# A spare PSUM column for the row maximum, the query ratio on GpSimd, and a strict order of all operations

## The chip, the cores and the metric

The kernel runs on one core of a Trainium2 chip. Five engines work side by side, each through its own queue in order: the matmul engine (PE, with its weight loads PEld), VectorE (DVE), ScalarE (ACT), GpSimd (POOL) and SyncE (SP), which issues most of the transfers. Data lies in SBUF, and matmuls write to PSUM, of which this kernel uses four tiles of two banks each. The metric is the device time of one execution in microseconds, as the median of several runs.

## The reference

A transformer layer on 2048 rows of 640: a linear attention with a learned feature map, then a bilinear gated FFN, each behind a layer norm and with a residual.

```python
x = A_x
h = x + _A_ref(_layernorm(x), A_wqkv, A_w_phi, A_wo)
h2 = h + _B_ref(_layernorm(h), B_w_gate, B_w_up, B_w_down)

# _A_ref, 32 heads of 20:
qkv = x @ wqkv                                # q, k, v
pq, pk = q @ w_phi[h], k @ w_phi[h]           # 20 x 20 per head
phi_q = concat(softmax(pq), softmax(-pq))     # 40 features
phi_k = concat(softmax(pk), softmax(-pk))
kv = sum_s phi_k[s] v[s];  z = sum_s phi_k[s]
o = (phi_q @ kv) / (phi_q @ z + 1e-6);  return o @ wo
# _B_ref: ((x @ w_gate) * (x @ w_up)) @ w_down, 1536 wide
```

## The kernel before

The 2048 rows are 16 tiles t of 128. Work is recorded as operations in named units, each on one engine; names carry the tile number.

- `s`: sums for the layer norm of a batch of tiles (PE and DVE, for batch s12 ACT squares), ending on POOL with `rs`, the reciprocal root (line 600). `x`, `y`: the key and query weights times w_phi. `c`: the value weights centred. `wo`: means of Wo's rows.
- `k`t: the key projection (ten matmuls of 128x320 into a PSUM tile), then `softexp`: DVE takes the negated largest magnitude of the row (`mx`, line 730) and multiplies it by `rs` (`nb`, line 733, both one column per partition), and ACT writes two exponentials, of plus and minus the row, with `nb` as bias (line 737). `K`t: DVE sums each group of 20 (line 748) and takes reciprocals (750), and POOL scales the key features with them (751).
- `v`t: the value projection, moved to SBUF by ACT. `A`t: the KV products of two tiles; all of them gather in one PSUM tile, which DVE moves to SBUF in unit `Aout` (817, 820).
- `q`t: query projection and `softexp`, into one of three `eq` buffers. `Q`t: DVE sums (770), a reciprocal (775) and the ratio of the two softmax sums (`rq`, line 776), then POOL scales half of the features with the ratio (781), and two DMA transposes bring them to `phiqT`.
- `n`t: the numerators, divided by DVE (848, 849) and transposed (by PE for tiles 0 and 1, else by DMA). `h`t: the product with Wo; DVE adds the residual (865 makes the mean column `mh`, 868 the sum), then a transpose, and the sum of squares on ACT and POOL.
- `f`b.i.j: FFN columns i for four tiles of block b (two tiles in block 0): five matmuls for the gate and five for the up half into the two banks of a PSUM tile; ACT copies the gate half (889), DVE multiplies (891). `d`t and `e`t: the product with w_down, scaling, residual and store.

Each row tile up to the KV eviction passes through PE, DVE, ACT and POOL; every numerator needs the KV product of all sixteen. From the first FFN unit on, PE has long runs of matmuls.

Which operation stands where on an engine is set when the program is built. `ORDER` lists unit names for each engine as ranks, and `Prog.place` walks through time with planned durations (`t`, `lat` of each operation): of the first four to six operations of an engine's list (`AHEAD`) it takes the first that can start by about the earliest possible time. Buffers from pools, the four PSUM tiles (`p_ps`) among them, are given out in that walk; a tile comes free when the last operation that names it in `use` has ended. The finished program has fixed queues, with semaphore waits where an operation needs another engine's result.

Of the kernel before, what the change touches and what calls it, by code (L numbers as in the profile page):

```python
# [5 lines left out]
FP32 = mybir.dt.float32  # L6
BF16 = mybir.dt.bfloat16
ACT = mybir.ActivationFunctionType
ALU = mybir.AluOpType
AX = mybir.AxisListType  # L10
# [26 lines left out]

SC = 175.0 / 128.0
# [23 lines left out]
    "DVE":  # L62
# [8 lines left out]
    "ACT":  # L71
# [7 lines left out]
    "POOL":  # L79
# [38 lines left out]
class Prog:  # L118
# [6 lines left out]
    AHEAD = {"PE": 4, "DVE": 6, "ACT": 6, "POOL": 4, "SP": 6}  # L125

    def __init__(self, nc, ctx):
        self.nc, self.ctx = nc, ctx
        self.ops = []
        self.rings = {}  # L130
        self.unit = None
        self.rank = {}
# [48 lines left out]
    def place(self):  # L181
# [3 lines left out]
        for o in ops:  # L185
            for d in o.deps:
                d.succ.append(o)
            o.open = len(o.deps)
            o.start = None
        free = {e: 0.75 for e in self.ENGS}  # L190
        fabric = 0.0
        for o in ops:
            self.rank.setdefault((o.eng, o.unit), len(self.rank))
        queue = {e: sorted((o for o in ops if o.eng == e), key=lambda o: (self.rank[e, o.unit], o.n)) for e in self.ENGS}
        flight = {}
        order = []
        wide = False
        while len(order) < len(ops):
            best = None
            for e in self.ENGS:  # L200
                cand, seen = [], 0
                for o in queue[e]:
                    if seen >= self.AHEAD[e] and not (wide and not cand):
                        break
                    seen += 1
                    if o.open:
                        continue
                    s = max([free[e]] + [d.end + (0.05 if d.eng != e else 0.0) for d in o.deps
                                         if d.eng != e or d.dma is not None or e not in ("PE", "SP")])
                    ok = True  # L210
                    for b in o.bufs:
                        if b.i is None:
                            if not b.pool.free:
                                ok = False
                                break
                            s = max(s, min(b.pool.free_at[j] for j in b.pool.free))
                    if ok and o.dma is not None:
                        fl = flight.get(o.dma[0], [])
                        if len(fl) >= o.dma[1]:
                            s = max(s, fl[-o.dma[1]])  # L220
                    if ok:
                        cand.append((s, o))
                if not cand:
                    continue
                s0 = min(c[0] for c in cand)
                s, o = next(c for c in cand if c[0] <= s0 + 0.06)
                if best is None or s < best[0]:
                    best = (s, o)
            if best is None:
                if wide:  # L230
                    raise RuntimeError("nothing can be placed")
                wide = True
                continue
            wide = False
# [25 lines left out]
            queue[o.eng].remove(o)  # L260
# [109 lines left out]
def _build(ctx, nc, A_x, A_wqkv, A_w_phi, A_wo, B_w_gate, B_w_up, B_w_down, out):  # L370
    g = Prog(nc, ctx)

    def sb(shape, dt, name):
        return ctx.enter_context(nc.sbuf_tensor(name, shape, dt))
# [37 lines left out]
    mx = sb([P, 2 * NT], FP32, "mx")  # L412
# [316 lines left out]
    def softexp(v, t, i, dst, regs_, use=()):  # L729
        g.op("DVE", lambda e: e.tensor_reduce(out=mx[:, i:i + 1], in_=PS[v.i][:, :, 0:HALF], axis=AX.XY, op=ALU.max,  # L730
                                              apply_absolute_value=True, negate=True), rd=v.R, wr=[R_mx[i]], use=[v],
             t=0.735, lat=0.85)
        g.op("DVE", lambda e: e.tensor_tensor(out=nb[:, i:i + 1], in0=mx[:, i:i + 1], in1=rs[:, t:t + 1], op=ALU.mult),  # L733
             rd=[R_mx[i], R_rs[t]], wr=[R_nb[i]], t=0.1, lat=0.2)
        for s in range(2):
            sc = rs if s == 0 else nrs
            g.op("ACT", lambda e, s=s, sc=sc: e.activation(  # L737
                out=signed(dst(), s), in_=PS[v.i][:, :, 0:HALF].rearrange("p b (h f) -> p b h f", f=DH), func=ACT.Exp,
                bias=nb[:, i:i + 1], scale=sc[:, t:t + 1]), rd=v.R + [R_nb[i], R_rs[t], R_nrs[t]], wr=[regs_[s]], use=[v] + list(use),
                t=0.775, lat=0.92)  # L740
# [21 lines left out]
    def queries(t, after=()):  # L762
# [10 lines left out]
        def sums(k):  # L773
            return Sq[:, vs.i, :].rearrange("p (h s) -> p h s", s=2)[:, :, k]
        g.op("DVE", lambda e: e.reciprocal(out=rq[:, vr.i, :], in_=sums(1)), rd=vs.R, wr=vr.R, use=[vs, vr], t=0.26, lat=0.38)
        g.op("DVE", lambda e: e.tensor_tensor(out=rq[:, vr.i, :], in0=sums(0), in1=rq[:, vr.i, :], op=ALU.mult),  # L776
             rd=vs.R + vr.R, wr=vr.R, use=[vs, vr], t=0.11, lat=0.2)
# [220 lines left out]
    for e, names in ORDER.items():  # L998
        for i, n in enumerate(names.split()):
            g.rank[e, n] = i  # L1000
# [29 lines left out]
```

## Time and profile before

| | |
|---|---|
| median of 3 runs | 298.22 us (298.15 to 298.28) |
| profiled execution | 298.66 us, its span 296.9 us |
| PE busy | 282.0 us, 2346 matmuls |
| DVE busy | 185.7 us, 302 instructions |
| ACT busy | 136.8 us |
| POOL busy | 104.6 us |
| granted TensorE clock, mean | 0.994 |

The span runs from the first to the last instruction; the profiled time has 1.8 us around it. In the page's rows stand the line, engine and operation, what is written and read, shapes and count; then busy time and the mean of one, and the engine's idle time just before with what ended it. In the window rows each engine has its busy time and its count; behind them stand the granted clock (1.00 is full speed), the share of the DMA engines and GB/s. Rows of waits give the total in us, how often, and the longest. Most tiles are parts of larger buffers, so names repeat: the FFN's matmuls show as `phik,Wgu`, since their input lies in the buffer that held the keys.

### The profile page before, as it was taken

What the parts mean: (1) busy time and instruction counts of PE and PEld (TensorE: products, weight loads), DVE (VectorE), ACT (ScalarE), POOL (GpSimd) and SP (SyncE); (2) the same over time, 40 slices, a digit from 0 to 9 for tenths busy, and PEclk for the clock granted to TensorE, in tenths of its full rate; (3) what the DMA queues carried; (4) which work ended last, traced back from release to release, by engine and by line L of the source; (5) the groups of instructions that cost most, each with busy time, mean ns of one, the idle gap of its engine ahead of it and who ended that gap; (6) DMA issues with size and microseconds to landing.
All of it is one profiled execution on the core that took longest, in us unless ns stands there. A gap on an engine that the chain in (4) does not pass through costs nothing.

```text
span 296.9 us, 5723 instructions
## 1 busy us (share of the span) xinstructions
PE 282.0 (95%) x2346; PEld 192.5 (65%) x2357; DVE 185.7 (63%) x302; ACT 136.8 (46%) x226; POOL 104.6 (35%) x143
## 2 busy tenths in 40 slices
PE   8999999787967999999999999999999999999996
PEld 8877677464866788978765466667654444456773
DVE  0799999999997989988775657352213232323201
ACT  1457897667834856526445213253332323223121
POOL 8426898663861154041252200151540000001042
PEclk9999999999998999999999999999999999999999
DMA  7978999600162587525434412518120000001111
GB/s 196 198 102 166 186 343 374 240 0 0 24 93 64 165 214 111 92 66 112 101 56 112 90 44 46 92 44 129 50 66 2 0 0 0 2 0 44 46 44 66
DMA packets 65193, 28.08 MB, mean 95 GB/s; under 512 B 55696, under 2 KB 63888, under 8 KB 65168
## 3 DMA queue, kind: packets, MB, share of 16 engines
q1 hardware_dynamic: 64240, 27.37, 40.7%
q10 hardware_dynamic: 928, 0.35, 0.5%
q8 instruction: 18, 0.29, 0.4%
q14 instruction: 7, 0.06, 0.1%
HBM read 11.82 MB, written 2.62 MB: 49 GB/s over the span
## 4 chain that ended last, share of the span: by engine, by line
PE 72%; DVE 21%; issue 3%; DMA 1%; POOL 1%; SPq 0%; ACT 0%; DVEq 0%; ACTq 0%; POOLq 0%
PE ps L553 71%; DVE Ssum L748 6%; DVE mx L730 4%; DVE nb L733 3%; DVE Rk L750 2%; DVE Sq L770 1%; DMA phiqT<-eq 1%; DVE rq L776 1%; PE ps L636 1%; DVE ob L849 1%; DVE Wp L684 0%; POOL eq L781 0%; DVE sxx L590 0%; DVE t L587 0%; SPq L462 0%
## 5 line engine op out<-in xcount | busy, mean ns | idle before, releaser
L553 PE MATMUL ps<-phik,Wgu 128*128 128x512 bf16 (+1 forms) x590 | 105.3, 336 | 0.5
L553 PEld LDWEIGHTS ps<-phik,Wgu 128*128 128x128 bf16 x600 | 58.3, 98 | 44.7 <-issue 0.2
L553 PE MATMUL ps<-Wp,xT 128*128 128x320 bf16 x480 | 69.9, 301 | 3.8 <-ACT eq L737 2.3
L891 DVE TENSOR_TENSOR phik<-ps,gate 128x512 bf16<-128x512 f32 (+1 forms) x60 | 34.8, 583 | 51.6 <-PE ps L553 50.5
L889 ACT ACTIVATE gate<-ps 128x512 bf16<-128x512 f32 (+1 forms) x60 | 30.6, 512 | 73.1 <-PE ps L553 73.1
L553 PE MATMUL ps<-vaug,phik 128*128 128x320 bf16 (+3 forms) x543 | 60.6, 273 | 2.3 <-POOL phik L751 2.2
L553 PEld LDWEIGHTS ps<-Wp,xT 128*128 128x128 bf16 x480 | 45.9, 98 | 22.9 <-ACT eq L737 3.0
L553 PEld LDWEIGHTS ps<-vaug,phik 128*128 128x128 bf16 x544 | 44.3, 100 | 18.2 <-POOL phik L751 2.4
L907 POOL TENSOR_TENSOR outb<-t,x_all 128x640 bf16<-128x640 f32 x12 | 16.7, 1397 | 83.2 <-ACT t L904 79.3
L751 POOL TENSOR_TENSOR phik<-phik,Rk 128x1280 bf16<-128x1280 bf16 x16 | 37.5, 2355 | 12.4 <-DVE Rk L750 12.0
L781 POOL TENSOR_TENSOR eq<-eq,rq 128x640 bf16<-128x640 bf16 x16 | 20.3, 1269 | 60.2 <-DVE rq L776 37.6
L730 DVE TENSOR_REDUCE mx<-ps 128x1 f32<-128x640 f32 x32 | 25.8, 807 | 1.8 <-PE ps L553 1.7
L904 ACT ACTIVATE t<-ps,mh,rs 128x640 f32<-128x640 f32 x12 | 10.5, 882 | 32.7 <-PE ps L553 29.1
L770 DVE TENSOR_REDUCE Sq<-eq 128x64 f32<-128x1280 bf16 x16 | 23.6, 1476 | 1.5 <-ACT eq L737 1.5
L748 DVE TENSOR_REDUCE Ssum<-phik 128x64 f32<-128x1280 bf16 x16 | 23.4, 1462 | 0.0
L737 ACT ACTIVATE eq<-ps,nb,rs 128x640 bf16<-128x640 f32 x16 | 14.1, 882 | 10.7 <-DVE nb L733 10.4
L737 ACT ACTIVATE phik<-ps,nb,rs 128x640 bf16<-128x640 f32 x16 | 14.1, 884 | 9.6 <-DVE nb L733 9.6
L546 ACT ACTIVATE junk<-x_all 128x640 bf16<-128x640 bf16 x20 | 14.6, 729 | 7.0 <-DVE x_all L868 6.9
L733 DVE TENSOR_TENSOR nb<-mx,rs 128x1 f32<-128x1 f32 x32 | 15.5, 489 | 0.9 <-POOL rs L600 0.5
L757 ACT ACTIVATE vaug<-ps,rs 128x640 bf16<-128x640 f32 x16 | 12.8, 799 | 4.3 <-PE ps L553 4.1
L868 DVE SCALAR_TENSOR_TENSOR x_all<-ps,mh,x_all 128x640 bf16<-128x640 f32 x16 | 14.1, 883 | 0.8
L865 DVE TENSOR_TENSOR mh<-ps,mv 128x1 f32<-128x1 f32 x16 | 2.5, 155 | 19.0 <-PE ps L553 18.9
(78 smaller groups left out, 258.0 us busy)
## 6 DMA issues: line engine op xcount, KB each, us to landing
x_all<-in_A_x_dram SPq DMA_DIRECT2D x4, 640.0 KB, 13.2
out_dram<-outb SPq DMA_DIRECT2D x15, 160.0 KB, 1.8
Wgu<-in_B_w_gate_dram SPq DMA_DIRECT2D x1, 1920.0 KB, 12.1
Wgu<-in_B_w_up_dram SPq DMA_DIRECT2D x1, 1920.0 KB, 14.2
vaug<-in_B_w_down_dram SPq DMA_DIRECT2D x1, 1920.0 KB, 8.4
Wp<-in_A_wqkv_dram SPq DMA_DIRECT2D x1, 800.0 KB, 5.2
phiqT<-in_A_wqkv_dram SPq DMA_DIRECT2D x1, 800.0 KB, 6.4
Wo<-in_A_wo_dram SPq DMA_DIRECT2D x1, 800.0 KB, 7.6
```

Source lines behind the costliest of these rows:

```text
L546: g.op("ACT", lambda e: e.activation(out=junk[:, v.i, :], in_=in_, func=func, accum_out=acc), rd=rd, wr=wr, use=[v], t=0.73, lat=0.97)
L553: ins = e.matmul(o_, lhsT=l_, rhs=r_, start=s_, stop=p_, skip_group_check=True)
L730: g.op("DVE", lambda e: e.tensor_reduce(out=mx[:, i:i + 1], in_=PS[v.i][:, :, 0:HALF], axis=AX.XY, op=ALU.max, apply_absolute_value=True, ...
L733: g.op("DVE", lambda e: e.tensor_tensor(out=nb[:, i:i + 1], in0=mx[:, i:i + 1], in1=rs[:, t:t + 1], op=ALU.mult), rd=[R_mx[i], R_rs[t]], w ...
L737: g.op("ACT", lambda e, s=s, sc=sc: e.activation(out=signed(dst(), s), in_=PS[v.i][:, :, 0:HALF].rearrange("p b (h f) -> p b h f", f=DH), ...
L748: g.op("DVE", lambda e: e.tensor_reduce(out=Ssum[:, vs.i, :], in_=x, axis=AX.X, op=ALU.add), rd=R_phik[t], wr=vs.R, use=[vs], t=1.39, lat=1.5)
L751: g.op("POOL", lambda e: e.tensor_tensor(out=x, in0=x, in1=Rk[:, vr.i, :].unsqueeze(2).to_broadcast([P, 2 * H, DH]), op=ALU.mult), rd=vr.R ...
L770: g.op("DVE", lambda e: e.tensor_reduce(out=Sq[:, vs.i, :], in_=eq[:, b.i, :].rearrange("p (g f) -> p g f", f=DH), axis=AX.X, op=ALU.add), ...
L781: return e.tensor_tensor(out=x, in0=x, in1=rq[:, vr.i, :].unsqueeze(2).to_broadcast([P, H, DH]), op=ALU.mult)
L889: g.op("ACT", lambda e: e.activation(out=gate[:, vg.i, 0:P * n], in_=PS[v.i][:, 0, 0:P * n], func=ACT.Copy), rd=[v.R[0]], wr=vg.R, use=[v, ...
L891: g.op("DVE", lambda e: e.tensor_tensor(out=hhT[:, hb, ft, sl], in0=PS[v.i][:, 1, 0:P * n], in1=gate[:, vg.i, 0:P * n], op=ALU.mult), rd=[ ...
L907: g.op("POOL", lambda e: e.tensor_tensor(out=outb[:, vo.i, :], in0=t32[:, v3.i, :], in1=x_all[:, t, :], op=ALU.add), rd=v3.R + [R_h[t]], w ...
```

## The change

- `softexp` drops the SBUF tensor `mx`. The reduction writes its column into column 400 (`MXC`) of the second bank of the projection's own PSUM tile, of which the projection fills 320 columns. `nb` reads it there; it now names the PSUM tile in `use`.
- The ratio `rq` of a query tile (line 776, now 778) goes from DVE to POOL, ahead of the scaling that uses it.
- `place` has no look-ahead: `ORDER` now lists a unit's name once for each of its operations, and each engine takes exactly the next in its list. The lists are new, for all five engines.

```diff
+MXC = 400
 ORDER = {
     "PE":
-        "s0 k1 wk x3 x1 wv x4 x0 q1 x2 k2 s2 k0 s4 k3 k5 k4 s8 v8 k7 A6 v1 k11 k8 wm v5 v3 v9 v10 k6 k14 s12 y1 v11 A4 "
...
+        "f2.8.0 f3.5.0 f3.3.0 f3.11.0 f3.10.0 f3.5.0 f3.10.0 f3.0.0 f3.3.0 f3.11.0 f2.9.0 f3.4.0 f3.0.0 f2.9.0 f3.9.0 "
...
-    AHEAD = {"PE": 4, "DVE": 6, "ACT": 6, "POOL": 4, "SP": 6}
...
     def place(self):
...
+            queue[e] = [units[n].pop(0) for n in self.order[e].split()]
...
             for e in self.ENGS:
-                cand, seen = [], 0
-                for o in queue[e]:
-                    if seen >= self.AHEAD[e] and not (wide and not cand):
-                        break
...
-                s0 = min(c[0] for c in cand)
-                s, o = next(c for c in cand if c[0] <= s0 + 0.06)
+                if head[e] == len(queue[e]) or queue[e][head[e]].open:
                     continue
+                o = queue[e][head[e]]
...
-    mx = sb([P, 2 * NT], FP32, "mx")
...
     def softexp(v, t, i, dst, regs_, use=()):
-        g.op("DVE", lambda e: e.tensor_reduce(out=mx[:, i:i + 1], in_=PS[v.i][:, :, 0:HALF], axis=AX.XY, op=ALU.max,
+        mx = lambda: PS[v.i][:, 1, MXC:MXC + 1]
+        g.op("DVE", lambda e: e.tensor_reduce(out=mx(), in_=PS[v.i][:, :, 0:HALF], axis=AX.XY, op=ALU.max,
                                               apply_absolute_value=True, negate=True), rd=v.R, wr=[R_mx[i]], use=[v],
              t=0.735, lat=0.85)
-        g.op("DVE", lambda e: e.tensor_tensor(out=nb[:, i:i + 1], in0=mx[:, i:i + 1], in1=rs[:, t:t + 1], op=ALU.mult),
-             rd=[R_mx[i], R_rs[t]], wr=[R_nb[i]], t=0.1, lat=0.2)
+        g.op("DVE", lambda e: e.tensor_tensor(out=nb[:, i:i + 1], in0=mx(), in1=rs[:, t:t + 1], op=ALU.mult),
+             rd=[R_mx[i], R_rs[t]], wr=[R_nb[i]], use=[v], t=0.1, lat=0.24)
...
-        g.op("DVE", lambda e: e.tensor_tensor(out=rq[:, vr.i, :], in0=sums(0), in1=rq[:, vr.i, :], op=ALU.mult),
-             rd=vs.R + vr.R, wr=vr.R, use=[vs, vr], t=0.11, lat=0.2)
+        g.op("POOL", lambda e: e.tensor_tensor(out=rq[:, vr.i, :], in0=sums(0), in1=rq[:, vr.i, :], op=ALU.mult),
+             rd=vs.R + vr.R, wr=vr.R, use=[vs, vr], t=0.3)
```

In the rows below, lines 731 and higher of the changed kernel stand one or two lower than in the kernel before.

DVE, the last operations ahead of and including the KV eviction. Before:

```order
L748 TENSOR_REDUCE Ssum<-phik 128x64
L750 RECIPROCAL Rk<-Ssum 128x64
L730 TENSOR_REDUCE mx<-ps 128x1
L733 TENSOR_TENSOR nb<-mx,rs 128x1
L730 TENSOR_REDUCE mx<-ps 128x1
L733 TENSOR_TENSOR nb<-mx,rs 128x1
L770 TENSOR_REDUCE Sq<-eq 128x64
L775 RECIPROCAL rq<-Sq 128x32
L776 TENSOR_TENSOR rq<-Sq,rq 128x32
L817 TENSOR_TENSOR KVsb<-ps,Gk 128x20x20
```

And now:

```order
L750 TENSOR_REDUCE Ssum<-phik 128x64
L752 RECIPROCAL Rk<-Ssum 128x64
L732 TENSOR_REDUCE ps<-ps 128x1
L735 TENSOR_TENSOR nb<-ps,rs 128x1
L772 TENSOR_REDUCE Sq<-eq 128x64
L777 RECIPROCAL rq<-Sq 128x32
L772 TENSOR_REDUCE Sq<-eq 128x64
L732 TENSOR_REDUCE ps<-ps 128x1
L735 TENSOR_TENSOR nb<-ps,rs 128x1
L819 TENSOR_TENSOR KVsb<-ps,Gk 128x20x20
L777 RECIPROCAL rq<-Sq 128x32
L822 SCALAR_TENSOR_TENSOR KVsb<-ps,Gk 128x20
```

The last key (unit K13 now, K15 before) is followed by the same kinds of operations, the ratio rq is gone, the maximum is written to PSUM, and one reciprocal stands between the parts of the KV eviction.

POOL, from the end of the last layer norm batch to the first query tiles. Before:

```order
L602 TENSOR_SCALAR nrs<-rs 128x4
L604 TENSOR_SCALAR mv<-sm 128x4
L751 TENSOR_TENSOR phik<-phik,Rk 128x1280 x8
L781 TENSOR_TENSOR eq<-eq,rq 128x32x20
L751 TENSOR_TENSOR phik<-phik,Rk 128x1280
L781 TENSOR_TENSOR eq<-eq,rq 128x32x20 x2
L751 TENSOR_TENSOR phik<-phik,Rk 128x1280
```

And now:

```order
L603 TENSOR_SCALAR nrs<-rs 128x4
L753 TENSOR_TENSOR phik<-phik,Rk 128x1280 x6
L778 TENSOR_TENSOR rq<-Sq,rq 128x32
L783 TENSOR_TENSOR eq<-eq,rq 128x32x20
L778 TENSOR_TENSOR rq<-Sq,rq 128x32
L783 TENSOR_TENSOR eq<-eq,rq 128x32x20
L753 TENSOR_TENSOR phik<-phik,Rk 128x1280 x3
L778 TENSOR_TENSOR rq<-Sq,rq 128x32
L783 TENSOR_TENSOR eq<-eq,rq 128x32x20
```

Before, one and two query scalings stood ahead of the last two key scalings; now two pairs of ratio and scaling stand ahead of the last three.

PE, from the last key and value projections (`Wp,xT`) over the KV products (`vaug,phik`, 128x84) to the first numerators (`KVsb,phiqT`). Before:

```order
L553 MATMUL ps<-Wp,xT 128x320 x70
L553 MATMUL ps<-vaug,phik 128x84 x60
L553 MATMUL ps<-Wp,xT 128x320 x40
L553 MATMUL ps<-vaug,phik 128x84 x100
L553 MATMUL ps<-Wp,xT 128x320 x10
L553 MATMUL ps<-KVsb,phiqT 128x84 x20
L475 MATMUL ps<-ident,ob 128x128 x5
L553 MATMUL ps<-KVsb,phiqT 128x84 x10
L475 MATMUL ps<-ident,ob 128x128 x5
```

And now, the last part of it:

```order
L554 MATMUL ps<-vaug,phik 128x84 x10
L554 MATMUL ps<-Wp,xT 128x320 x10
L554 MATMUL ps<-vaug,phik 128x84 x50
L554 MATMUL ps<-Wp,xT 128x320 x10
L554 MATMUL ps<-KVsb,phiqT 128x84 x20
L554 MATMUL ps<-Wp,xT 128x320 x10
L476 MATMUL ps<-ident,ob 128x128 x10
L554 MATMUL ps<-KVsb,phiqT 128x84 x10
```

The KV products are now mixed with projections, and a query projection stands both ahead of the first two numerators (q6) and between them and their transposes (q7).

More of the change, by code (lines that the diff above doesn't have):

```diff
@@ L131, in __init__ @@
         self.unit = None
-        self.rank = {}
+        self.order = {}
     def op(self, eng, emit, rd=(), wr=(), app=(), dma=None, t=0.2, lat=None, use=(), after=(), size=0.0):
@@ L188, in place @@
             o.open = len(o.deps)
-            o.start = None
         free = {e: 0.75 for e in self.ENGS}
         fabric = 0.0
-        for o in ops:
-            self.rank.setdefault((o.eng, o.unit), len(self.rank))
-        queue = {e: sorted((o for o in ops if o.eng == e), key=lambda o: (self.rank[e, o.unit], o.n)) for e in self.ENGS}
+        queue, head = {}, {e: 0 for e in self.ENGS}
+        for e in self.ENGS:
+            units = {}
+            for o in ops:
+                if o.eng == e:
+                    units.setdefault(o.unit, []).append(o)
+            queue[e] = [units[n].pop(0) for n in self.order[e].split()]
+            if any(units.values()):
+                raise RuntimeError("operations without a place")
         flight = {}
         order = []
-        wide = False
         while len(order) < len(ops):
@@ L200, in place @@
             for e in self.ENGS:
-                cand, seen = [], 0
-                for o in queue[e]:
-                    if seen >= self.AHEAD[e] and not (wide and not cand):
-                        break
[L205 to L223, printed above, removed]
-                    continue
-                s0 = min(c[0] for c in cand)
-                s, o = next(c for c in cand if c[0] <= s0 + 0.06)
+                if head[e] == len(queue[e]) or queue[e][head[e]].open:
+                    continue
+                o = queue[e][head[e]]
+                if any(b.i is None and not b.pool.free for b in o.bufs):
+                    continue
+                s = max([free[e]] + [d.end + (0.05 if d.eng != e else 0.0) for d in o.deps
+                                     if d.eng != e or d.dma is not None or e not in ("PE", "SP")])
+                for b in o.bufs:
+                    if b.i is None:
+                        s = max(s, min(b.pool.free_at[j] for j in b.pool.free))
+                if o.dma is not None:
+                    fl = flight.get(o.dma[0], [])
+                    if len(fl) >= o.dma[1]:
+                        s = max(s, fl[-o.dma[1]])
                 if best is None or s < best[0]:
@@ L229, in place @@
             if best is None:
[L230 to L234, printed above, removed]
+                raise RuntimeError("the orders of the engines block each other")
             s, o = best
@@ L259, in place @@
             order.append(o)
-            queue[o.eng].remove(o)
+            head[o.eng] += 1
             for x in o.succ:
@@ L997, in _build @@
             fd(t)
-    for e, names in ORDER.items():
-        for i, n in enumerate(names.split()):
-            g.rank[e, n] = i
+    g.order = ORDER
     g.finish()
```

68 rows, old and new, of the table ORDER are left out of this document.

## The prediction

> **What bounds the kernel now.** I read the share of each engine over the span first, then the slices, then what the matmul engine (PE) waited for, and last the rows of the VectorE (DVE) queue where PE waits.
>
> ```profile
> PE 282.0 (95%) x2346; PEld 192.5 (65%) x2357; DVE 185.7 (63%) x302; ACT 136.8 (46%) x226; POOL 104.6 (35%) x143
> PE   8999999787967999999999999999999999999996
> DVE  0799999999997989988775657352213232323201
> PEclk9999999999998999999999999999999999999999
> PE 72%; DVE 21%; issue 3%; DMA 1%; POOL 1%; SPq 0%; ACT 0%; DVEq 0%; ACTq 0%; POOLq 0%
> ```
>
> PE is busy for 95% of the span, yet there are two stages. From slice 13 on (about 97 us) PE has no hole; ahead of that DVE stands at 9 and PE drops to 7 or 6. The chain of waits says the same: its 21% of DVE all lie ahead of 97 us. Windows over the three parts (PE's columns come first):
>
> ```profile
> core 0: us, PE busy (x) PEld busy (x) DVE busy (x) ACT busy (x) POOL busy (x), PEclk, DMA share, GB/s
> 1.04:93.14 92.10, 82.77 (x934) 64.36 (x934) 81.65 (x115) 60.68 (x92) 60.40 (x82) 0.98 0.66 157
> 93.14:104.33 11.19, 9.98 (x111) 7.47 (x112) 9.92 (x20) 7.35 (x12) 1.28 (x2) 1.00 0.56 152
> 104.33:293.49 189.16, 188.58 (x1296) 120.19 (x1307) 93.12 (x166) 68.81 (x123) 42.50 (x56) 1.00 0.29 61
> ```
>
> 93.14 is where the first numerator (unit n) starts, 104.33 the first FFN unit (f). The last 189 us hold nothing to win: PE is 99.7% busy. All PE's waits up to 104.33, one row per cause:
>
> ```profile
> PE ps L553 <- ACT phik L737: 2.9, 4, 1.4
> PE ps L553 <- ACT eq L737: 2.3, 2, 1.4
> PE ps L553 <- POOL phik L751: 2.2, 1, 2.2
> PE ps L475 <- DVE ob L849: 1.2, 2, 0.9
> PE ps L553 <- POOL ones L512: 1.0, 1, 1.0
> PE ps L553 <- DVE sm L583: 0.7, 1, 0.7
> PE ps L553 <- DVE Wp L684: 0.6, 1, 0.6
> PE ps L553 <- DVE KVsb L820: 0.4, 1, 0.4
> PE ps L553 <- DVE outb L618: 0.2, 1, 0.2
> ```
>
> They come to 11.5 us; the 1.0 for the ones at the start stays, 10.5 us in 13 waits can go. Who makes ACT and GpSimd (POOL) late is told by the group of the small product nb:
>
> ```profile
> L733 DVE TENSOR_TENSOR nb<-mx,rs 128x1 f32<-128x1 f32 x32 | 15.5, 489 | 0.9 <-POOL rs L600 0.5
> L865 DVE TENSOR_TENSOR mh<-ps,mv 128x1 f32<-128x1 f32 x16 | 2.5, 155 | 19.0 <-PE ps L553 18.9
> 52.96 2.35 POOL L751 TENSOR_TENSOR phik<-phik,Rk 128x1280 bf16<-128x1280 bf16 x1 [0.56 <-DVE Rk L750]
> 53.59 1.74 DVE L733 TENSOR_TENSOR nb<-mx,rs 128x1 f32<-128x1 f32 x1
> 195.14 2.75 POOL L907 TENSOR_TENSOR outb<-t,x_all 128x640 bf16<-128x640 f32 x2
> 195.21 0.16 DVE L865 TENSOR_TENSOR mh<-ps,mv 128x1 f32<-128x1 f32 x1 [0.29 <-PE ps L553]
> ```
>
> One column per partition takes 489 ns on average where mh, as small, takes 155. In the pair of timeline rows the product starts at 53.59 and ends at 55.33, within 0.02 us of the end of POOL's operation (52.96 + 2.35 = 55.31): it stands still until POOL is done. nb reads two tensors in SBUF. mh reads one in PSUM and one in SBUF, and at 195.21 it took 0.16 us in the middle of a POOL operation that ran from 195.14 on. So the stretch hangs on the second SBUF read.
>
> **The change, part by part.** *nb.* In the stage where DVE is full, from its first instruction to the KV eviction, the windows of lines 733 and 776 are:
>
> ```profile
> 8.57:91.88 83.31, 13.95 (x21) 0.98 0.65 150
> 8.57:91.88 83.31, 2.47 (x4) 0.98 0.65 150
> ```
>
> 21 nb take 13.95 us; at mh's 155 ns they would take 3.3, so 10.7 us leave DVE's queue. The maximum is now written to PSUM and read from there by nb. No row shows a reduction that writes PSUM. Below, it costs nothing; above, I bound it by one more small PSUM operation per maximum, 155 ns x 21 = 3.3 us. I take nothing, since mh is the nearest row and its PSUM read is no longer than nb's unstretched 0.16. [...]
>
> *Query ratio.* The four rq of line 776 leave DVE: 2.47 us. On POOL each becomes an operation on 128x32. POOL's rows on either side:
>
> ```profile
> L593 POOL TENSOR_TENSOR msq<-sm 128x4 f32<-128x4 f32 x3 | 0.6, 201 | 4.0 <-DVE sm L583 4.0
> L781 POOL TENSOR_TENSOR eq<-eq,rq 128x640 bf16<-128x640 bf16 x16 | 20.3, 1269 | 60.2 <-DVE rq L776 37.6
> 27.07:88.04 60.97, 45.79 (x34) 1.00 0.58 161
> ```
>
> Between 201 ns for 4 columns and 1269 for 640, 32 columns lie at about 0.25 us (1.68 ns a column); 0.2 and 1.27 are the ends, and 0.25 is the value, being next to the small one. All sixteen make 4 us on an engine that is 35% busy, but two of them now stand on POOL ahead of the last three key scalings (phik, line 751), whose result the KV product waits for. From its first scaling at 27.07 to the end of its last at 88.04 POOL worked 45.8 us (the window above); with 0.5 more it could be through at 73.4. That is hidden as long as PE reaches its last KV products later than this.
>
> *The stage's new end.* DVE: 91.88 - 10.7 - 2.5 = 78.7 us for the KV eviction, its other idle time kept. PE: the first n at 93.14, less its waits until then (10.5 - 1.2 for ob = 9.3), less what the waits cost beside. That is a fill and a cold clock:
>
> ```profile
> 49.71 4.24 PE L553 MATMUL ps<-Wp,xT 128*128 128x320 bf16 x30
> 54.17 1.53 PE L553 MATMUL ps<-Wp,xT 128*128 128x320 bf16 x10 [0.22 <-ACT phik L737]
> 83.40 2.45 PE L553 MATMUL ps<-vaug,phik 128*128 128x84 bf16 x60
> 88.09 2.59 PE L553 MATMUL ps<-vaug,phik 128*128 128x84 bf16 x40 [2.24 <-POOL phik L751]
> 88.59:92.00 3.41, 3.41 (x38) 2.77 (x35) 2.51 (x6) 2.80 (x5) 0.05 (x1) 0.50 0.21 48
> ```
>
> 20 matmuls more take 2.71 us, so ten are 1.36 and each group that begins after a wait carries 0.175 of fill that a gapless stream hides: 13 x 0.175 = 2.3 us, 1.9 of it ahead of 93.14. And after the 2.24 us hole at 85.85 the granted clock was 0.50 for 3.41 us: 1.7 us lost, and indeed 40 matmuls took 2.59 where 60 had taken 2.45. So PE could reach n at 93.14 - 9.3 - 1.9 - 1.7 = 80.2, 1.5 us later than DVE: the bound passes from DVE to PE, and no more than PE's own loss can be won. That is 10.5 + 2.3 + 1.7 = 14.5 us. [...]
>
> *The order.* Every operation has a fixed place now, and PE's stages interleave. The waits that the stretch didn't cause (rows ob, sm, KVsb and outb above) come to 2.5 us in five, with fills 3.4. The new order places q6 and q7 around n0 and n1, which covers ob and KVsb; but it has tight places of its own: POOL's scalings behind two ratios, ACT's four squares of batch s12 now ahead of the exponentials of k5 and waiting for a load, and PSUM tiles taken again after one half unit of f. Below, nothing new; I let it have 3.4 us, as much as the old order had. On SP one load of x_all moves ahead of the query weights' transposes, one between the two halves of Q0's transpose, one behind Q12's.
>
> ```profile
> x_all<-in_A_x_dram SPq DMA_DIRECT2D x4, 640.0 KB, 13.2
> phiqT<-eq SPq DMA_TRANSPOSE x32, 2.5
> ```
>
> The loads have 10 us and more until they are used, and are costed at nothing; if Q0's second half lands behind its load, 13.2 instead of 2.5 us after issue, n0 comes some 8 us late: that is in the second case below.
>
> *Sum.* The profiled execution took 298.66 us, its span 296.9. 298.66 - 14.5 + 3.4 = 287.6; it lies 0.44 above the median of the three runs, so **287.2 us**.
>
> **The rivals.** *Lockstep.* With DVE ending 1.5 us ahead of PE, and ACT, 60.7 us busy of the 92 ahead of 93.14, doing the same in some 79, queues that wait in turn keep PE waiting for ACT as often as now: 5.2 us in six waits plus 1.1 of fill, 293.5. For it: ACT and DVE serve strictly in their queues. Against it: each of these waits ended on an exponential that waited for a stretched nb. *Another cold stretch.* By the row at 88.59, one more hole like that costs 2.2 + 0.2 + 1.7 = 4.1 us: 291.3. *The stretch remains,* because DVE and POOL exclude each other whatever nb reads: DVE keeps its 10.7 us and the time is about 297. Row 195.21 speaks against it. *Slower: tiles held too long.* PE has four PSUM tiles, and in the FFN the new order opens up to four f units before it closes the first; the tile closed first is taken again after one half unit.
>
> ```profile
> L891 DVE TENSOR_TENSOR phik<-ps,gate 128x512 bf16<-128x512 f32 x36 | 24.9, 691 | 49.0 <-PE ps L553 48.9
> L553 PE MATMUL ps<-phik,Wgu 128*128 128x512 bf16 x350 | 77.3, 379 | 0.5
> ```
>
> Half a unit is 5 of these matmuls, 5 x 77.3/350 = 1.10 us of cover; the drain is 0.69 plus the fill, 0.87 us. A drain that is late by one more product (0.69) stalls PE by 0.25 to 0.5. At 0.25 for each of the 60 units, 15 us, the time is 302; it decides above 14.5 - 3.4 = 11 us, 0.19 a unit. Against it: the margin is there, and DVE worked 93 of these 189 us.
>
> **How the numbers follow.** Forecast 0.66 (its own range 284.5 to 290: no new wait at all gives 283.8, twice the allowance 290.6); lockstep 0.16; cold stretch 0.07; stretch remains 0.06; tiles held 0.05. 284.5 to 293.0 leaves out a little at the low end, half of the lockstep and the last two cases: 2 in 10. Of the case at 297 I count two thirds as faster, as 0.2% (0.6 us, what a measurement of this kernel tells from no change) is soon passed, the rest as the same or slower. Faster 0.93, same 0.02, slower 0.05.
>
> **What would show it.** nb at about 155 ns with no value above 0.3; sixteen rq on POOL near 0.25 us; the first KVsb matmul at 80 to 84 us; PEclk 9 in all slices; less than 5 us of waits on PE, with f to the last matmul again 189 us. Wrong if nb still ends with POOL's operations; if PE's list shows ACT or POOL with 5 us; or if waits for phik L893 (the f product) appear after 100 us.

## The result and the profile after

The changed kernel takes **285.15 us** (median of 4 runs, 284.99 to 285.51), the kernel before 298.25 us beside it (4 runs, 298.15 to 298.33): a ratio of 0.9563, with a 95% interval of 0.9546 to 0.9579. The forecast was 287.2 us, with a range of 284.5 to 293.0, so the result stands near its low end. The profiled execution took 285.01 us and its span is 283.3 us, 13.6 us shorter than the span before. Every line of the changed kernel that the rows name stands one or two lower, those ahead of 731 too: the matmuls of line 553 are on 554.

The page of the changed kernel: busy time of the engines, the slices of two of them with the granted clock, and the chain of waits by engine.

```profile
PE 277.4 (98%) x2344; PEld 191.4 (68%) x2357; DVE 165.7 (59%) x286; ACT 134.3 (47%) x226; POOL 108.2 (38%) x159
PE   8999999999999999999999999999999999999996
DVE  0799998999889888685765554621331232324011
PEclk9999999999999999999999999999999999999999
PE 96%; DVE 1%; ACT 1%; issue 0%; POOL 0%; POOLq 0%
```

PE has no slice below 9 between the first and the last, and DVE, which stood at 9 for ten slices in a row, now drops to 8 among them. The chain has passed from 21% DVE to 1%. The same three parts as before, cut at the first numerator and the first FFN unit:

```profile
core 0: us, PE busy (x) PEld busy (x) DVE busy (x) ACT busy (x) POOL busy (x), PEclk, DMA share, GB/s
1.04:80.15 79.11, 78.37 (x933) 63.16 (x934) 67.67 (x111) 59.84 (x92) 60.37 (x84) 1.00 0.71 174
80.15:90.95 10.80, 10.14 (x112) 7.51 (x110) 9.72 (x19) 6.67 (x11) 1.19 (x3) 1.00 0.21 47
90.95:279.90 188.95, 188.26 (x1296) 120.32 (x1307) 87.34 (x157) 67.78 (x124) 46.18 (x69) 1.00 0.33 71
```

The first part lost 13.0 us (92.10 to 79.11), the second 0.4, the FFN 0.2. All that PE waited for in the whole span:

```profile
PE ps L554 <- POOL ones L513: 1.0, 1, 1.0
PE ps L554 <- ACT phiqT L644: 0.4, 1, 0.4
PE ps L476 <- DVE ob L851: 0.4, 1, 0.4
PE ps L554 <- ACT Wp L682: 0.3, 1, 0.3
PE ps L554 <- ACT phik L479: 0.2, 1, 0.2
```

Of the nine causes the wait for the ones at the start is left, a rest of ob, and three small new ones. The groups of the operations that were edited, and two rows of the timeline like those that showed the stretch:

```profile
L735 DVE TENSOR_TENSOR nb<-ps,rs 128x1 f32<-128x1 f32 x32 | 4.2, 134 | 0.5 <-POOL rs L601 0.3
L778 POOL TENSOR_TENSOR rq<-Sq,rq 128x32 f32<-128x32 f32 x16 | 4.0, 253 | 64.7 <-DVE rq L777 64.7
L732 DVE TENSOR_REDUCE ps<-ps 128x1 f32<-128x640 f32 x32 | 26.1, 819 | 4.6 <-PE ps L554 4.3
...
70.73 4.67 POOL L753 TENSOR_TENSOR phik<-phik,Rk 128x1280 bf16<-128x1280 bf16 x2 [0.32 <-DVE nb L735]
73.36 0.16 DVE L735 TENSOR_TENSOR nb<-ps,rs 128x1 f32<-128x1 f32 x1
```

nb fell from 489 to 134 ns, and the one that starts at 73.36, in the middle of two scalings of POOL, is through in 0.16 us. In the stage where DVE was full, the windows of nb alone are now:

```profile
8.57:78.32 69.75, 2.52 (x21) 1.00 0.68 165
```

21 nb took 13.95 us before; they take 2.52, so 11.4 us have left DVE's queue there.

### The profile page after: what moved, and what is told of

It is laid out like the page before. It is cut to its first block, busy times and chain, and to the rows that moved or that the text cites. A ratio compares the mean times of both kernels' runs of the same rounds, so it can differ in the third digit from the quotient of the medians.

```text
span 283.3 us, 5691 instructions
## 1 busy us (share of the span) xinstructions
PE 277.4 (98%) x2344; PEld 191.4 (68%) x2357; DVE 165.7 (59%) x286; ACT 134.3 (47%) x226; POOL 108.2 (38%) x159
## 4 chain that ended last, share of the span: by engine, by line
PE 96%; DVE 1%; ACT 1%; issue 0%; POOL 0%; POOLq 0%
PE ps L554 96%; DVE ob L851 1%; PE ps L637 1%; PE ps L476 0%; DVE outb L934 0%; ACT Wp L682 0%; ACT phiqT L644 0%; ACT phik L479 0%; DVE rden L850 0%; POOL ones L513 0%; POOLq L1015 0%
## 5 line engine op out<-in xcount | busy, mean ns | idle before, releaser
L893 DVE TENSOR_TENSOR phik<-ps,gate 128x512 bf16<-128x512 f32 (+1 forms) x60 | 34.1, 578 | 60.6 <-PE ps L554 41.8
L891 ACT ACTIVATE gate<-ps 128x512 bf16<-128x512 f32 (+1 forms) x60 | 29.9, 510 | 66.0 <-PE ps L554 55.3
L732 DVE TENSOR_REDUCE ps<-ps 128x1 f32<-128x640 f32 x32 | 26.1, 819 | 4.6 <-PE ps L554 4.3
L778 POOL TENSOR_TENSOR rq<-Sq,rq 128x32 f32<-128x32 f32 x16 | 4.0, 253 | 64.7 <-DVE rq L777 64.7
L876 POOL TENSOR_SCALAR vpe<-shc 128x1 f32<-128x1 f32 x16 | 3.0, 191 | 32.4 <-ACT junk L547 31.5
L739 ACT ACTIVATE phik<-ps,nb,nrs 128x640 bf16<-128x640 f32 x16 | 14.2, 890 | 0.0
## 6 DMA issues: line engine op xcount, KB each, us to landing
Wgu<-in_B_w_gate_dram SPq DMA_DIRECT2D x1, 1920.0 KB, 11.3
```

The costliest lines, as they stand in the source:

```text
L732: g.op("DVE", lambda e: e.tensor_reduce(out=mx(), in_=PS[v.i][:, :, 0:HALF], axis=AX.XY, op=ALU.max, apply_absolute_value=True, negate=Tru ...
L739: g.op("ACT", lambda e, s=s, sc=sc: e.activation(out=signed(dst(), s), in_=PS[v.i][:, :, 0:HALF].rearrange("p b (h f) -> p b h f", f=DH), ...
L891: g.op("ACT", lambda e: e.activation(out=gate[:, vg.i, 0:P * n], in_=PS[v.i][:, 0, 0:P * n], func=ACT.Copy), rd=[v.R[0]], wr=vg.R, use=[v, ...
L893: g.op("DVE", lambda e: e.tensor_tensor(out=hhT[:, hb, ft, sl], in0=PS[v.i][:, 1, 0:P * n], in1=gate[:, vg.i, 0:P * n], op=ALU.mult), rd=[ ...
```

## The experiments

The theory: an nb or rq that reads two SBUF tensors stands still while POOL works; by this DVE set the end of the part ahead of the KV eviction; without it PE sets the end. The main rival: the new order of all queues makes the gain, and the stretch was hidden anyway. Since the change has three parts (the maximum in PSUM, the ratio on POOL, the order), the first six experiments run all the combinations that were left. PE begins with 48 products of a tile of ones, the warm-up. Below, "after the warm-up" is the time from the first product behind it (line 554, `ps<-ones,phiqT`) to the first product with KVsb. In the kept traces the warm-up ends between 5.05 and 6.14 us, and in two traces of one program at 6.14 and 5.33, so this distance compares better than the span. For the changed kernel it is 80.15 - 5.57 = 74.58 us, from these rows of the timeline:

```profile
5.57 0.27 PE L554 MATMUL ps<-ones,phiqT 128*128 128x1 bf16 x5
80.15 0.94 PE L554 MATMUL ps<-KVsb,phiqT 128*128 128x84 bf16 x20
```

For the kernel before it is 93.14 - 6.14 = 87.00 us. The eight combinations and the run with a pointer scalar in one table; ratios are to the kernel before, run on the same chip:

| order | maximum | ratio rq | median, us | ratio, 95% interval | nb, mean ns | after the warm-up, us |
|---|---|---|---|---|---|---|
| before | SBUF | DVE | 298.25 | 1 | 489 | 87.00 |
| before | SBUF | POOL | 294.95 | 0.9875 (0.9848 to 0.9903) | 504 | 84.09 |
| before | PSUM | DVE | 287.44 | 0.9614 (0.9586 to 0.9643) | 140 | 76.54 |
| before | PSUM | POOL | 285.96 | 0.9555 (0.9521 to 0.9590) | 139 | 75.14 |
| new | SBUF | DVE | 293.11 | 0.9799 (0.9770 to 0.9829) | 403 | 82.11 |
| new | SBUF | POOL | 290.68 | 0.9739 (0.9711 to 0.9767) | 451 | 80.45 |
| new | PSUM | DVE | 286.09 | 0.9574 (0.9544 to 0.9604) | 136 | 75.75 |
| new | PSUM | POOL | 285.15 | 0.9563 (0.9546 to 0.9579) | 134 | 74.58 |
| new | SBUF, pointer scalar | POOL | 285.43 | 0.9549 (0.9520 to 0.9579) | 179 | 74.85 |

### The maximum in PSUM, in the order of before

```diff
-        g.op("DVE", lambda e: e.tensor_reduce(out=mx[:, i:i + 1], in_=PS[v.i][:, :, 0:HALF], ...
+        mx = lambda: PS[v.i][:, 1, 400:401]
+        g.op("DVE", lambda e: e.tensor_reduce(out=mx(), in_=PS[v.i][:, :, 0:HALF], ...
-        g.op("DVE", lambda e: e.tensor_tensor(out=nb[:, i:i + 1], in0=mx[:, i:i + 1], in1=rs[:, t:t + 1], ...
+        g.op("DVE", lambda e: e.tensor_tensor(out=nb[:, i:i + 1], in0=mx(), in1=rs[:, t:t + 1], ...
```

Every queue keeps its order.

> The kernel before, with its own order of every queue, and one edit: the row maximum is written to the spare PSUM column and nb reads it there. Theory (nb stood still on VectorE because its two operands lay in SBUF while GpSimd worked): nb falls from 489 ns to about 155 ns, VectorE delivers earlier, TensorE's waits shrink, 288.5 us (287 to 290). Rival (the gain is the new order's; the stretch of nb is hidden anyway): 296 to 298 us.

Measured: 287.44 us, 0.9614, as the theory had it. The group of nb in this kernel:

```profile
L733 DVE TENSOR_TENSOR nb<-ps,rs 128x1 f32<-128x1 f32 x32 | 4.3, 140 | 0.9 <-POOL rs L599 0.5
```

So 11.3 of the 13.1 us (against 298.72 us for the kernel before on the same chip) come from two lines of code, with no instruction moved. The rival, that the order makes the gain, falls: it gave 296 or more.

### Both edits, in the order of before

The same edit, and rq goes from DVE's place to POOL, directly ahead of the scaling that reads it; nothing else.

```diff
+        order = moved(order)
...
-        g.op("DVE", lambda e: e.tensor_tensor(out=rq[:, vr.i, :], in0=sums(0), in1=rq[:, vr.i, :], op=ALU.mult),
+        o_rq = g.op("DVE", lambda e: e.tensor_tensor(out=rq[:, vr.i, :], in0=sums(0), in1=rq[:, vr.i, :], op=ALU.mult),
...
-        g.op("POOL", f, rd=vr.R + [b.R[1]], wr=[b.R[1]], use=[b, vr], t=1.25)
+        MOVED.append((o_rq, g.op("POOL", f, rd=vr.R + [b.R[1]], wr=[b.R[1]], use=[b, vr], t=1.25)))
```

> The order of before, row maximum in PSUM, and the query ratio moved to GpSimd directly ahead of the scaling that reads it; nothing else moves. Theory: 287 us (285.5 to 289), and what is left against the changed kernel, 0 to 3 us, is what the new order adds. Rival (the order makes the gain): 296 to 298 us.

Measured: 285.96 us, 0.9555, inside the theory's range and as fast as the changed kernel within the intervals. What the new order adds was measured once more on one chip, further below.

### The new order with neither edit

```diff
+    mxs = sb([P, 2 * NT], FP32, "mx")
...
-        mx = lambda: PS[v.i][:, 1, MXC:MXC + 1]
+        mx = lambda: mxs[:, i:i + 1]
...
-        g.op("POOL", lambda e: e.tensor_tensor(out=rq[:, vr.i, :], in0=sums(0), ...
+        g.op("DVE", lambda e: e.tensor_tensor(out=rq[:, vr.i, :], in0=sums(0), ...
```

In the lists, each query tile has its third place on DVE again, behind its reciprocal, and one place less on POOL.

> The order of the changed kernel, with both operations as they were before: row maximum in SBUF, query ratio on VectorE directly behind its reciprocal. Theory: nb is stretched again (mean about 490 ns), VectorE sets the end of the keys' part, 297 us (294 to 300). Rival (the order makes the gain): about 285 us, as the changed kernel.

Measured: 293.11 us, 0.9799. Both missed: the order gives 5 to 6 us by itself, where the theory gave it about 1, and it doesn't give 13. The group of nb shows part of the reason:

```profile
L735 DVE TENSOR_TENSOR nb<-mx,rs 128x1 f32<-128x1 f32 x32 | 12.8, 403 | 0.5 <-POOL rs L601 0.3
...
8.57:86.40 77.83, 10.64 (x21) 1.00 0.61 147
```

The new order doesn't take the stretch away, but nb meets POOL's operations less: up to the KV eviction its 21 take 10.64 us (the second row, the window of nb alone), 3.3 less than before. And the 2.24 us hole ahead of the last KV products is gone with the half clock behind it (1.7 us; the granted clock is 1.00 in every slice here). Of the 5.5 us of span, 4.9 lie ahead of the first numerator (87.00 to 82.11 us after the warm-up). The two make 5.0 us, about as much; that just these two make the gain is argued, and no run tells them apart. So the gains of order and edits do not add up: each of them shrinks the same loss, and the gain of the order is 5.5 us without the edits and about 1 with them.

### The new order with the maximum in PSUM, rq on DVE

The third hunk above, without the first two.

> The order of the changed kernel, row maximum in PSUM, query ratio on VectorE. Theory: nb near 150 ns, rq as long as before (about 790 ns, stretched by GpSimd), but most of the 16 rq stand in the feed-forward part where VectorE has room; 286 us (285 to 287.5). Rival (rq on VectorE matters as much as nb): 288 us and above.

Measured: 286.09 us, 0.9574, as the theory had it. The 790 ns that it gave rq have no row behind them: rq took 363 ns on average in the kernel before, and 302 here. Most are not stretched (median 192 ns), but one of those ahead of the KV eviction is, for 1.96 us. rq on DVE costs about 1 us beside the changed kernel.

### The order of before with rq on POOL alone

The edit of "both edits" without the maximum in PSUM.

> The order of before, row maximum in SBUF as before, and only the query ratio moved to GpSimd directly ahead of the scaling that reads it. Theory: nb is stretched as before (15.5 us in 32), four rq leave VectorE in the keys' part (2.5 us there); 296 us (295 to 297). Rival (the order and the GpSimd work decide, VectorE's queue does not): 298 us or more, since GpSimd gets 16 operations more.

Measured: 294.95 us, 0.9875, by the interval 2.9 to 4.5 us faster than before; the theory's range, 295 to 297, is just missed at its low end. The wait of 2.24 us behind which PE's clock had fallen to 0.50 is shorter here. Two rows of PE's timeline, and a window that holds the hole between them (the third figure from the right is the granted clock):

```profile
83.52 2.45 PE L570 MATMUL ps<-vaug,phik 128*128 128x84 bf16 x60
87.29 1.70 PE L570 MATMUL ps<-vaug,phik 128*128 128x84 bf16 x40 [1.32 <-POOL phik L768]
...
80.00:100.00 20.00, 17.48 (x239) 13.85 (x237) 18.56 (x31) 11.65 (x20) 8.61 (x9) 1.00 0.49 110
```

After a hole of 1.32 us the clock stayed at 1.00, and 40 matmuls took 1.70 us, where they had taken 2.59 after the hole of 2.24.

### The changed kernel with the maximum back in SBUF

The first two hunks of "neither edit" alone; rq stays on POOL.

> The changed kernel with one thing undone: the row maximum goes to an SBUF tile again, so nb reads two SBUF tensors; query ratio on GpSimd, order of the changed kernel. By what the changed kernel's order with neither edit showed (KVsb 8.1 us later, of which nb 7.9 us), theory: 292 us (291 to 293.5), nb at about 11 us up to the KVsb copies. Rival (rq on VectorE carried half of that loss): 289 us or less.

Measured: 290.68 us, 0.9739, below the theory's range of 291 to 293.5 and above the rival's 289: neither was right. The stretch is back, as the group and one pair of the timeline show:

```profile
L735 DVE TENSOR_TENSOR nb<-mx,rs 128x1 f32<-128x1 f32 x32 | 14.3, 451 | 0.5 <-POOL rs L601 0.3
...
32.36 4.67 POOL L753 TENSOR_TENSOR phik<-phik,Rk 128x1280 bf16<-128x1280 bf16 x2
34.81 2.24 DVE L735 TENSOR_TENSOR nb<-mx,rs 128x1 f32<-128x1 f32 x1
...
8.57:84.00 75.43, 11.85 (x21) 1.00 0.63 152
```

The nb that starts at 34.81 ends at 37.05; POOL's pair ends at 32.36 + 4.67 = 37.03. Up to the KV eviction nb costs 11.85 us (the last row, the window of nb alone) against 2.52, 9.3 more, yet the first product with KVsb is only 80.45 - 74.58 = 5.9 us later. By this, DVE in the changed kernel has some 3.4 us of room for a delay of this kind, more than the 1.5 us of the forecast.

### One SBUF tensor and a pointer scalar

This kernel tells whether the second *tensor* is what counts, or any second read from SBUF. The maximum stays in SBUF, and the other factor becomes a per-partition pointer scalar, also in SBUF:

```diff
-        g.op("DVE", lambda e: e.tensor_tensor(out=nb[:, i:i + 1], in0=mx(), in1=rs[:, t:t + 1], op=ALU.mult),
+        g.op("DVE", lambda e: e.tensor_scalar(out=nb[:, i:i + 1], in0=mx(), scalar1=rs[:, t:t + 1], scalar2=None, op0=ALU.mult),
```

> As the run before this one (row maximum in SBUF), but nb is a tensor_scalar: one SBUF tensor as operand, the other factor as a per-partition pointer scalar, also in SBUF. Theory A (what stalls is a second tensor operand): nb at 0.1 to 0.2 us, 285.3 us (284.8 to 286). Theory B (any second SBUF read stalls, or any VectorE operation stalls beside GpSimd): nb stretched up to 2 us, 292 us.

Measured: 285.43 us, 0.9549: theory A. Group and pair:

```profile
L735 DVE TENSOR_SCALAR nb<-mx,rs 128x1 f32<-128x1 f32 x32 | 5.7, 179 | 0.5 <-POOL rs L601 0.3
...
71.56 4.67 POOL L753 TENSOR_TENSOR phik<-phik,Rk 128x1280 bf16<-128x1280 bf16 x2 [0.28 <-DVE nb L735]
74.21 0.21 DVE L735 TENSOR_SCALAR nb<-mx,rs 128x1 f32<-128x1 f32 x1
```

All operands lie in SBUF, POOL works all around it, and nb takes 0.21 us. In this run the pointer scalar does not act as a second input. The other nb say the same. In the kernel before, nine nb start while POOL scales keys, and every one ends within 0.04 us of the end of a scaling; in the changed kernel 13 start under a scaling of keys or queries and none lasts over 0.16 us; with the pointer scalar 12 do up to 80 us of its span, and none lasts over 0.21.

### More work on DVE

Behind each of the last eight keys' reciprocals (`LATE`) stands one more, which nothing reads.

```diff
+        if t in LATE:
+            for _ in range(1):
+                g.op("DVE", lambda e: e.reciprocal(out=spare[:, LATE.index(t), :], in_=mhalf[:, 0:1].to_broadcast([P, 2 * H])), ...
```

> The changed kernel with eight reciprocals more on VectorE (128x64 fp32, about 0.47 us each, 3.8 us in all), one behind each of the last eight keys' own reciprocals; nothing reads them. Theory (the bound passed from VectorE to TensorE with a margin of about 1.5 us): the keys' part ends 2.3 us later, 287.4 us (286.6 to 288). Rival 1 (VectorE still sets the end): all 3.8 us, 288.9 us. Rival 2 (VectorE has much room): 285.2 us.

Measured: 286.76 us, 0.9604 (0.9577 to 0.9630), 0.6 us below the theory's figure and inside its range.

```profile
L755 DVE RECIPROCAL spare<-mhalf 128x64 f32<-128x64 f32 x8 | 4.0, 494 | 0.0
81.38 0.95 PE L554 MATMUL ps<-KVsb,phiqT 128*128 128x84 bf16 x20
```

4.0 us more on DVE move the first numerator to 81.38 - 5.26 = 76.12 us after the warm-up, 1.5 us later. The bound has passed from DVE to PE, with 2.5 us of room here by busy time. On DVE the next operation starts ahead of a reciprocal's end: in the kernel before, one of 0.54 us starts at 52.34 and its successor at 52.80, 0.08 us before that end. With the same overlap 0.494 us fill 0.41, an estimate, so the eight fill 3.3 us of its queue, and by that the room is 1.8 us. In the run with rq on DVE, the four rq ahead of the first numerator took 2.5 us and made it 1.2 us later, so 1.3 us of room were left there. The room thus depends on where the work falls, from 1.3 to 3.4 us in these runs.

### The last scaling late

Ahead of the scaling of the last key, number 13, POOL does two more of the same size, into a tile that nothing reads.

```diff
+        if t == 13:
+            for k in range(2):
+                g.op("POOL", lambda e, k=k: e.tensor_tensor(out=spare..., in0=(spare... if k else x), in1=Rk[:, vr.i, :]..., op=ALU.mult), ...
```

> The changed kernel with two scalings more on GpSimd (2.35 us each, into a tile that nothing reads) ahead of the last key's scaling, which then ends about 4.7 us later; the margin there is about 1.5 us, so TensorE stands for about 3.2 us ahead of the last products of the keys' part. Theory (a hole of that length costs 1.7 us of half clock behind it, as a hole of 2.24 us did in the kernel before): 290 us (289.3 to 290.8), granted clock 0.50 for about 3.4 us. Rival (the clock holds through such a hole): 288.4 us (287.8 to 289), granted clock 1.00 throughout.

Measured: 290.47 us, 0.9719 (0.9684 to 0.9754). PE's timeline around the hole, and the window of half clock:

```profile
76.03 1.52 PE L554 MATMUL ps<-Wp,xT 128*128 128x320 bf16 x10
80.70 3.39 PE L554 MATMUL ps<-vaug,phik 128*128 128x84 bf16 x50 [3.15 <-POOL phik L756]
...
81.09:84.50 3.41, 3.41 (x48) 3.18 (x45) 1.31 (x4) 0.00 (x0) 2.59 (x3) 0.50 0.21 48
```

A hole of 3.15 us, and behind it 3.41 us at a clock of 0.50: the same length as in the kernel before. The first numerator comes 85.55 - 6.08 = 79.47 us after the warm-up, 4.9 later than in the changed kernel; 3.15 + 1.7 = 4.85. So a cold stretch costs what the prediction gave it, and the margin of POOL's last scaling is 1.6 us, where 1.5 had been expected: it ends 4.7 us later, and PE waits 3.15. This is its row on POOL:

```profile
78.28 2.36 POOL L756 TENSOR_TENSOR phik<-phik,Rk 128x1280 bf16<-128x1280 bf16 x1
```

It ends at 80.64, 74.56 us after the warm-up, where the changed kernel's pair (70.73 + 4.67) ends 69.83 after it.

### Three kernels side by side

What the order and the pointer scalar are worth beside the changed kernel is about 1 us or less, so the three ran together.

> The order of before with both edits once more, beside the changed kernel on the same chip, for what the new order adds by itself when both edits are there. Theory (by the first profile of this kernel: first product with KVsb 0.56 us later after the warm-up than in the changed kernel, and 0.31 us more from there to the feed-forward part): 0.9 us above the changed kernel. Rival (the order adds nothing): within 0.3 us of it.

> The changed kernel itself, on the same chip as the two beside it: 285.2 us (284.9 to 285.6).

> The row maximum in SBUF with nb as a tensor_scalar with a pointer scalar, beside the changed kernel. Theory (its 45 ns more per nb cost TensorE next to nothing, since VectorE has room; by its first profile the first product with KVsb is 0.27 us later after the warm-up): 0 to 0.4 us above the changed kernel. Rival (23 nb of 45 ns stand on the path): 1.0 us above.

Measured: 286.08 us (0.9585, 0.9564 to 0.9605) for the old order with both edits, 284.87 us (0.9545, 0.9528 to 0.9563) for the changed kernel, 285.10 us (0.9550, 0.9532 to 0.9568) for the pointer scalar. The intervals of the first two lie just apart; the earlier pair, 0.9555 and 0.9563 on different chips, stood the other way round, so the order's own share lies between nothing and 1.2 us. The traces put 0.4 us of it ahead of the first numerator (74.97 against 74.57 us after the warm-up) and 0.35 between the numerators and the FFN (11.15 against 10.80). The pointer scalar cannot be told from the changed kernel, as its theory had it. The changed kernel itself came out 0.03 us below the range expected of it.

## Why the prediction was right

**The sum.** It was 298.66 - 14.5 + 3.4 = 287.6 for the profiled execution; 285.01 was measured, 2.6 less. The term that was mis-sized is the *allowance for waits of the new order*: 3.4 us were given, and the trace has four waits of 1.3 us together, with the forecast's 0.175 of fill each 2.0. That is 1.4 of the 2.6. Another 0.6 is the end of the warm-up, 6.14 before and 5.57 after, which differs as much between executions of one kernel (6.14 and 5.33 above). The remaining 0.6 lies ahead of the first numerator: 80.2 - 6.14 = 74.1 us after the warm-up, and 1.05 for the two waits that fell there with their fills, make 75.1, where 74.58 was measured. What made it shorter wasn't traced.

**nb.** Forecast 155 ns with none above 0.3 us, and 10.7 us off DVE's queue; 134 ns, none above 0.16 us, and 11.4 measured. Shortest, median and longest nb before and after, in ns:

```profile
L733 DVE TENSOR_TENSOR nb<-mx,rs x32: 90/159/2053, 18.2 to 178.6; 128x1 f32<-128x1 f32 x32
...
L735 DVE TENSOR_TENSOR nb<-ps,rs x32: 93/148/159, 17.5 to 161.9; 128x1 f32<-128x1 f32 x32
```

The mechanism held in both orders: 489 to 140 ns with not one instruction moved. From PSUM nb was no slower than unstretched from SBUF: 93 against 90 ns at the short end, 148 against 159 in the median, though the latter has nine held-up nb in it.

**The maximum in PSUM** was taken at no cost, with 155 ns as the upper bound: the reduction went from 807 to 819 ns, 0.25 us for 21.

**rq.** 0.25 us on POOL was forecast, 0.253 measured. POOL was to be through with the keys at 73.4 and was at 75.40 (70.73 + 4.67), but PE needed it 1.6 us later still, as the run with the late scaling shows.

**DVE 78.7, PE 80.2.** The KV eviction began at 78.32, the first numerator at 80.15. Both had the warm-up end as before; it ended 0.6 us earlier. That the bound passes to PE is shown by the eight reciprocals. The margin of 1.5 us was misread: it sets the start of the KV eviction on DVE against the first numerator on PE, and the eviction itself takes 1.26 us (91.88 to 93.14 before), so the forecast's own rows leave 0.3. The runs show 1.3 to 3.4. Part of it is waiting of DVE's own that the forecast did not see: up to the first numerator DVE waits 1.3 us for PE ahead of maxima and 0.7 for ACT ahead of a query's sum, and only 0.8 and nothing in the run with eight reciprocals more. That the bound passed with room to spare was not foreseen, then; by the forecast's rows, DVE 0.4 us slower would have kept it. And not all of the chain's DVE lay ahead of 97 us: 1.0 us of it, 0.3% of the span, stands at the kernel's end (line 932).

**The clock.** 1.00 throughout, and 1.7 us were rightly counted as recoverable: the run with the late scaling pays just this. Without that term the sum would have been 287.2 + 1.7 = 288.9, further from the measurement.

**The order.** Its cover of ob and KVsb held: 0.4 us of ob is left. The loads of x_all that moved ahead in SP's queue landed in 4.9 us at the median instead of 13.2 and delayed nothing. What the prediction didn't see is that the order alone also thins out the stretch and closes the 2.24 us hole; that doesn't count in the sum, since the edits take both away.

**The rivals.** *Lockstep:* PE's waits for ACT are 0.9 us in three. The waiting went the other way: DVE now waits for PE ahead of the maxima, as its waits in the whole span show, before and after; up to the first numerator they are 0.3 and 1.3 us.

```profile
DVE mx L730 <- PE ps L553: 1.7, 4, 0.9
...
DVE ps L732 <- PE ps L554: 4.3, 7, 1.7
```

*Cold stretch:* none here, though the run with the late scaling has one behind its hole of 3.15 us. *The stretch remains:* refuted by the pairs of rows. *Tiles held too long:* the FFN took 188.95 us against 189.16.

## What to carry to other kernels

A tiny operation whose mean is several times that of another of its size (here 489 ns against 155), and which ends with another engine's operation (here within 0.04 us), is standing still, and what it delays is found behind it in its queue. Here it was a tensor_tensor on VectorE with both tensors in SBUF beside GpSimd work; one operand in PSUM, or a tensor_scalar with a pointer scalar in place of the second tensor, freed it: 134 and 179 ns on average, where two SBUF tensors in the same order took 451. The second is an edit of one line that needs no PSUM column; it was run in the new order with rq on POOL only. When several edits shrink one loss, price each of them with the others in place: the order was worth 5.5 us alone and at most 1.2 beside the two edits.

## What the runs showed of the hardware

- On VectorE, nb with one SBUF tensor and an SBUF pointer scalar was not held up by GpSimd (0.11 to 0.22 us in all 32), while the same product of two SBUF tensors lasted up to 2.24 us in the changed kernel with the maximum back in SBUF; in the kernel before, each of the nine that started under a GpSimd scaling of keys ended with a scaling, within 0.04 us.
- PE's clock fell to 0.50 after holes of 2.24 and 3.15 us and held after one of 1.32, and after one of 1.5 in the changed kernel with the maximum back in SBUF (1.00 there over 80 to 100 us). Behind both of the long holes it stayed down for 3.41 us, and the fall came 2.7 and 3.5 us after PE had stopped (85.85 to 88.59, 77.55 to 81.09), when PE had been working again for 0.4 to 0.5 us. The loss differed between executions: of the 30 of the kernel before that ran beside the experiments, 7 show a mean clock of 0.988 in place of 0.994 and took 299.4 to 299.8 us. Where they lost it, no kept trace shows.
